# Windowed attention and a gated MLP: two pairs of heads together, scores in three bursts, values in two

## The chip, the cores and the metric

The kernel runs on one core of one Trainium2 chip. The metric is the time on the device in microseconds (us) of one execution. Five engines work beside each other: TensorE (PE in the profile, its weight loads PEld), VectorE (DVE), ScalarE (ACT), GpSimd (POOL) and SyncE (SP, which here issues all loads and stores). Each runs its own instructions in order and waits for the others by semaphores.

## What is computed

Causal attention over a window of 128 keys with a slope per head, then an MLP whose second half is mixed over the sequence. Shapes: 8 batches, 8 heads, 576 positions, 64 dimensions a head; d_model 512, d_ff 1024. All in float32.

```python
scores = q @ k.T / sqrt(64) - slope[h] * |i - j|   # where 0 <= i - j < 128
attn = softmax(scores); x = attn @ v               # heads side by side: (8, 576, 512)
h = gelu_tanh(x @ w_in); u, v = halves of h
v_n = (v - mean) / sqrt(var + 1e-6) * g_ln         # over the 512 features
v_s = w_sg @ v_n + b_sg                            # over the 576 positions
out = x + (u * v_s) @ w_out
```

## The kernel before

*Attention, by pair of heads* (class Pair, 32 pairs, four to a batch). Queries are cut into 18 groups of 32. A group n needs the keys of five groups, n-4 to n, which are 160 columns; groups 0 to 3 need fewer. PE is used in tiles. For the scores, tiles of 64 rows (the 64 dimensions of one head) by 32 columns (the queries of a group): eight at a time, four groups ("quarters" g of the 128 output partitions) of both heads. For the values, tiles of 32 rows (32 keys, one quarter) by 64 columns (the dimensions of one head), eight as well. A pair has nine slots, each holding one group in each quarter: slots 0 to 4 (X) and 5 to 8 (Y); the first slot of each has the early groups 0 to 3 with 128 columns (padded with a bias), the others 160.

The steps of pair n, by the letters of the order below: `q` loads q and k, `L` loads v (five transfers a pair); `*` 36 score products into four banks of PSUM (72 matmuls in the trace, where each fp32 product of these tiles appears twice); `A B C G` on DVE subtract from the bias and take the row minimum (L281); `e E f F` exponentials on ACT with their sums (L286); `R` reciprocals; `s S` scaling on POOL (L297); `t T` transposes by 32 x 32 blocks on DVE (L301); `V` 80 value products, one for each group of 32 keys, quarter and head, with one to five groups of 32 queries as columns (160 matmuls, L331), into four banks; `x` copies the result to xf, `h l k` split it into a high and a low part (xs). The probabilities of a pair stand in one of three buffers e; qk and vt have two buffers each. A pair's score burst (`*`) and value burst (`V`) are each issued without a break.

*The MLP, by batch.* u and v from w_in (`u`, `v`, `tt`), normalisation (`n..`), mixing over the sequence (`y`, L687, L688), gating (`gm gh gl`), w_out (`O`, L540 to L542) and the sum with x (`oa`), store (`D`). Each product is three matmuls (high x high, high x low, low x high) on the whole array, of 288 columns or, for v and tt, of 512. A step of u or O has 12 matmuls, of y 14, of v 12 and of tt 8. The weights are split once at the start (`i d b + H -` and `w..`); `i` loads a quarter of a half of w_in or w_out.

*The order.* A planner collects every step with its engine, its needs and its buffers; the order in which the steps are issued is written out by hand (`ORDER`), and each engine follows it. ON_VECTOR names those copies and subtractions that DVE does instead of ACT or POOL. In the old order PE begins `*0 *1 *2 V0 *3 V1 *4 V2 *5`, then the first `v` of batch 0 between `V3`, `*6` and `V4`; it ends with `V31 V30` and the last MLP.

## Time and profile before

| | |
|---|---|
| median of 3 runs | 643.37 us (637.86 to 644.07) |
| the profiled execution | 642.52 us, its span 640.8 us |
| mean granted TensorE clock | 0.947 of full speed |
| busy: PE, PEld, DVE, ACT, POOL | 587.4, 541.0, 376.6, 355.0, 231.0 us |
| moved by DMA | 59.37 MB, mean 93 GB/s |

The span runs from the first to the last instruction of the profiled execution; its own time is 1.7 us more. Busy times count an engine's instructions, not its waits. Matmuls overlap in the records, so a start-to-start distance tells more than the length of one. "issue" as the reason of a wait means that the engine waited for nothing that the profile shows. [...]

### The profile page before, as it was taken

What the parts mean: (1) busy time and instruction counts of PE and PEld (TensorE: products, weight loads), DVE (VectorE), ACT (ScalarE), POOL (GpSimd) and SP (SyncE); (2) the same over time, 40 slices, a digit from 0 to 9 for tenths busy, and PEclk for the clock granted to TensorE, in tenths of its full rate; (3) what the DMA queues carried; (4) which work ended last, traced back from release to release, by engine and by line L of the source; (5) the groups of instructions that cost most, each with busy time, mean ns of one, the idle gap of its engine ahead of it and who ended that gap; (6) DMA issues with size and microseconds to landing.
All of it is one profiled execution on the core that took longest, in us unless ns stands there. A gap on an engine that the chain in (4) does not pass through costs nothing.

```text
span 640.8 us, 23707 instructions
## 1 busy us (share of the span) xinstructions
PE 587.4 (92%) x10304; PEld 541.0 (84%) x10304; DVE 376.6 (59%) x1211; ACT 355.0 (55%) x951; POOL 231.0 (36%) x197
## 2 busy tenths in 40 slices
PE   4569979999999999899989999999798998989997
PEld 3457867999998899797988999888797997988997
DVE  7668995377566676456736763547273466534422
ACT  6765968676452673558535874387281843512320
POOL 7666484174233212321612532424050542141020
PEclk9669998999999999899989999999697998979999
DMA  9984544501532323222324053432522022300103
GB/s 259 244 240 125 174 115 115 112 2 40 160 114 62 100 84 120 78 62 82 102 49 105 3 179 100 95 68 68 132 86 71 1 59 68 80 3 1 38 1 112
DMA packets 57564, 59.37 MB, mean 93 GB/s; under 512 B 4466, under 2 KB 47474, under 8 KB 57460
## 3 DMA queue, kind: packets, MB, share of 16 engines
q1 hardware_dynamic: 57460, 57.86, 33.0%
q8 instruction: 81, 1.33, 0.9%
q14 instruction: 23, 0.19, 0.1%
HBM read 48.40 MB, written 9.44 MB: 90 GB/s over the span
## 4 chain that ended last, share of the span: by engine, by line
PE 89%; issue 6%; DVE 1%; ACT 1%; POOL 1%; DMA 1%; POOLq 0%; SPq 0%; ACTq 0%
PE bank L540 22%; PE bank L541 21%; PE bank L542 21%; PE bank L331 13%; PE bank L266 8%; PE bank L688 1%; PE bank L687 1%; PE bank L623 1%; PE bank L625 1%; DMA wst<-w_in 1%; POOL g L702 1%; ACT e L286 1%; DVE e L301 0%; DVE e L281 0%; POOLq L870 0%
## 5 line engine op out<-in xcount | busy, mean ns | idle before, releaser
L286 ACT ACTIVATE e<-e,small 128x160 f32<-128x160 f32 (+1 forms) x288 | 118.0, 411 | 16.4 <-DVE small L281 16.0
L297 POOL TENSOR_TENSOR e<-e,small 128x640 f32<-128x640 f32 (+1 forms) x64 | 91.2, 1443 | 97.0 <-DVE small L290 87.7
L331 PEld LDWEIGHTS bank<-e,vt 32*64 32x64 f32 x5120 | 80.4, 143 | 47.7 <-issue 42.4
L331 PE MATMUL bank<-e,vt 32*64 32x32 f32 (+3 forms) x5120 | 86.5, 252 | 37.3 <-issue 30.4
L281 DVE CUSTOM_DVE_ANT_0 e<-bank,bias 128x160 f32<-128x160 f32 (+1 forms) x288 | 74.6, 308 | 23.0 <-PE bank L266 22.6
L564 POOL TENSOR_TENSOR small<-small 128x1 f32<-128x1 f32 (+1 forms) x40 | 30.1, 755 | 150.9 <-DVE small L561 145.8
L540 PE MATMUL bank<-ws,vn 128*128 128x288 f32 x256 | 79.6, 311 | 0.0
L702 POOL TENSOR_TENSOR g<-u,g 128x576 fp32r<-128x576 f32 x32 | 46.8, 1481 | 87.8 <-ACT g L699 87.6
L541 PE MATMUL bank<-ws,vn 128*128 128x288 f32 x256 | 78.0, 305 | 0.0
L542 PE MATMUL bank<-ws,vn 128*128 128x288 f32 x256 | 77.9, 304 | 0.0
L540 PE MATMUL bank<-xs,wi 128*128 128x288 f32 x256 | 77.4, 302 | 0.0
L540 PE MATMUL bank<-g,wo 128*128 128x288 f32 x256 | 76.7, 300 | 0.0
L542 PE MATMUL bank<-xs,wi 128*128 128x288 f32 x256 | 76.4, 298 | 0.0
L541 PE MATMUL bank<-xs,wi 128*128 128x288 f32 x256 | 76.3, 298 | 0.0
L541 PE MATMUL bank<-g,wo 128*128 128x288 f32 x256 | 75.7, 296 | 0.3 <-POOL g L702 0.3
L542 PE MATMUL bank<-g,wo 128*128 128x288 f32 x256 | 75.5, 295 | 0.0
L694 DVE TENSOR_TENSOR u<-bank,u 128x288 f32<-128x288 f32 x64 | 27.8, 448 | 81.1 <-PE bank L688 73.1
L266 PE MATMUL bank<-qk 64*32 64x160 f32 (+1 forms) x2304 | 60.4, 332 | 12.7 <-issue 5.9
L266 PEld LDWEIGHTS bank<-qk 64*32 64x32 f32 x2304 | 46.1, 120 | 21.6 <-issue 10.8
L301 DVE STREAM_TRANSPOSE e<-e 128x608 f32<-128x608 f32 (+1 forms) x64 | 55.7, 879 | 8.7 <-POOL e L297 8.6
L286 ACT ACTIVATION_READ_ACCUMULATOR e<-e,small 128x1 f32 x288 | 54.0, 187 | 0.0
L725 DVE TENSOR_TENSOR xf<-bank,xf 128x288 f32<-128x288 f32 x64 | 27.9, 449 | 41.5 <-PE bank L542 41.3
(97 smaller groups left out, 1312.3 us busy)
## 6 DMA issues: line engine op xcount, KB each, us to landing
qk<-qkT SPq DMA_DIRECT2D x32, 576.0 KB, 5.0
vt<-v_in SPq DMA_DIRECT2D x96, 128.0 KB, 3.4
outT<-xf SPq DMA_DIRECT2D x28, 288.0 KB, 2.3
vt<-v_in SPq DMA_DIRECT2D x32, 176.0 KB, 3.5
wst<-w_in SPq DMA_DIRECT2D x8, 512.0 KB, 6.9
vt<-v_in SPq DMA_DIRECT2D x32, 64.0 KB, 3.9
wst<-w_out SPq DMA_DIRECT2D x4, 512.0 KB, 5.6
wst<-w_sgT SPq DMA_DIRECT2D x4, 288.0 KB, 3.1
```

The lines of the kernel that those rows point to most:

```text
L266: return lambda: nc.tensor.matmul(self.place[s][quarter[g]], qk[heads[j], 0, n * Q:(n + 1) * Q], ks, start=True, stop=True)
L281: nc.vector.tensor_tensor_reduce(out=self.pr[:, s, skip:KW], in0=self.place[s], in1=bs, scale=-1.0 / math.sqrt(D), scalar=3e38, op0=ALU.ad ...
L286: nc.scalar.activation(x, x, AF.Exp, bias=self.nm[:, s:s + 1], scale=-1.0, accum_out=self.sm[:, s:s + 1])
L297: nc.gpsimd.tensor_tensor(x, x, self.rr[:, ss].rearrange("p (m o) -> p m o", o=1).broadcast_to(list(x.shape)), ALU.mult)
L301: nc.vector.transpose(x, x)
L331: insts.append(lambda x=x, at=at, n=len(mine): nc.tensor.matmul(*x, start=(at == 0), stop=(at == n - 1), skip_group_check=True))
L540: nc.tensor.matmul(dst, ah, bh, start=(first and i == 0), stop=False)
L541: nc.tensor.matmul(dst, ah, bl, start=False, stop=False)
L542: nc.tensor.matmul(dst, al, bh, start=False, stop=(last and i == n - 1))
L564: nc.gpsimd.tensor_tensor(x["rs"][0:rows], x["rs"][0:rows], mhalf[0:rows], ALU.pow)
L702: nc.gpsimd.tensor_tensor(st[f"g{f}"][:, 1, :], st["u"][:, f, :], st[f"g{f}"][:, 0, :].bitcast(F32), ALU.subtract)
L725: nc.vector.tensor_tensor(o, st[f"po{c}{i}"][:, 0:S2], o, ALU.add)
```

## The change

Two pairs of heads (a "Two", 16 of them) go through the softmax together. Each quarter g now holds, for one of the two pairs (g // 2), a run of seven groups that follow each other: groups 4 to 10 or 11 to 17. Two sets of slots (base 0 and 1, seven slots each, all of 160 columns) are the two heads. The early groups 0 to 3 of both pairs get four slots of their own (32, 64, 96 and 128 columns) in base 0. That makes 18 slots for two pairs, as before.

- Scores come in three bursts `*a *b *c` (slots 0 to 2, 3 to 5, 6 and the early ones) of 24 products each, 48 matmuls in the trace, two banks each; each burst has its own minima (`Aa Ba` ...), exponentials (`ea Ea` ...), reciprocals, scaling and transposes. The early slots are scaled on DVE (`z`, four operations), no longer on POOL.
- Values come in two bursts: `Va` takes the keys that need only parts a and b (48 products, 96 matmuls), `Vb` the rest (56 products, 112 matmuls). With seven consecutive groups a product has up to five groups of queries for most keys: 104 products for two pairs instead of 160. Both bursts write the same four banks, and the two pairs' `x` copy from them after `Vb`.
- v is loaded in six transfers for two pairs instead of ten. A load of q and k waits for all three bursts of the Two before; only Two 1 gets a buffer of its own, borrowed from vn. There are two buffers e and two vt, each for a Two.
- ON_VECTOR and ORDER are written anew. PE begins `*a0 *c0 *b0 *b1 *a1 *c1 Va0 Vb0 *a2 *b2 *c2`, then a first part of `v`, `Va1 Vb1 *a3 *c3`, the rest of `v` of batch 0, `*b3 tt0 Va2 Vb2 *c4 *b4 *a4`, three `y` and eight `u` steps, `Va3 Vb3`. From Two 4 on, Va and Vb stand next to each other on PE in six of twelve Twos.

The core of the diff; "..." marks what is left out, most of the order among it. Of the functions of Two, which take the place of those of Pair printed above, the new lines alone are shown.

```diff
+    RUN = (S // Q - NG) // 2
+    CUT = (0, 3, 6, RUN)
+    NS = 2 * RUN + NG
+    LATER = 2 * RUN * KW
+    EW = LATER + NG * 3 * Q + Q
...
+    def head_of(base, g):
+        return g // 2 if base == 0 else 1 - g // 2
+    def first_of(g):
+        return NG + g % 2 * RUN
+    def early_pair(g):
+        return (0, 1, 1, 0)[g]
...
+    class Two:
+        def __init__(self, d):
+            self.d, self.b, self.hp = d, 2 * d // NPAIR, 2 * d % NPAIR
+            self.nm, self.sm, self.rr = stats[d % 2]
             self.heads = [slice(j * D, (j + 1) * D) for j in range(2)]
+            self.pr = e_bufs[d % 2]
+            self.bias = biases[self.hp // 2]
+            self.qk, self.to = [None] * 2, {}
+        def load_qk(self, p):
+            if self.d == 1:
+                if p == 0:
+                    self.both = mlp.tile([P, 2, 2, S], F32, name="qk1", tag="vn")
+                x = self.both[:, p]
+            else:
+                x = att.tile([P, 2, S], F32, name="qk", bufs=2)
+            self.qk[p] = x
+            h = 2 * (self.hp + p)
+            nc.sync.dma_start(x, qkT[self.b, h:h + 2].rearrange("h d t s -> (h d) t s"))
         def load_v(self):
+            b, kv = self.b, NG + RUN
+            vt = self.vt = att.tile([P, kv + 2, 2 * D], F32, name="vt", bufs=2)
+            def rows(k, n, c, w):
+                return v[b, k * Q:(k + n) * Q, c:c + w].rearrange("(k p) d -> p k d", p=Q)
             for g in range(NG):
...
+                c0 = (self.hp + g // 2) * 2 * D
+                nc.sync.dma_start(vt[quarter[g], 0:kv], rows(first_of(g) - NG, kv, c0, 2 * D))
+                if g % 2:
+                    c0 = (self.hp + early_pair(g)) * 2 * D + head_of(0, g) * D
+                    nc.sync.dma_start(vt[quarter[g], kv:].rearrange("p i (j d) -> p (i j) d", j=2), rows(0, NG, c0, D))
...
+        def scores(self, k):
+            heads, work = self.heads, range(CUT[k], CUT[k + 1])
             insts = []
+            def score(x, base, g, p, n, keys):
+                j = head_of(base, g)
+                qk = self.qk[p]
+                ks = bass.AP(qk.tensor, qk.offset + S + (n + 1) * Q - keys, [list(qk.ap[0]), [1, keys]])[heads[j]]
+                insts.append(lambda: nc.tensor.matmul(x[quarter[g]], qk[heads[j], 0, n * Q:(n + 1) * Q], ks, start=True, stop=True))
+            at = [bank(), bank()]
+            for base in range(2):
+                for i in work:
+                    self.to[base, i] = at[base][:, (i - CUT[k]) * KW:(i - CUT[k] + 1) * KW]
+            for i in work:
                 for g in range(NG):
+                    for base in range(2):
+                        score(self.to[base, i], base, g, g // 2, first_of(g) + i, KW)
+            if k == 2:
+                c = len(work) * KW
+                for n in reversed(range(NG)):
+                    w = (n + 1) * Q
+                    x = self.to[2, n] = at[0][:, c:c + w]
+                    c += w
+                    for g in range(NG):
+                        score(x, 0, g, early_pair(g), n, w)
             burst(insts)
...
+        def slots(self, base, k):
+            for i in range(CUT[k], CUT[k + 1]):
+                c = (base * RUN + i) * KW
+                s = self.stat(base, i)
+                yield self.to[base, i], self.pr[:, c:c + KW], self.bias[:, base], slice(s, s + 1)
+            if k == 2 and base == 0:
+                for n in reversed(range(NG)):
+                    c, w, s = LATER + n * 3 * Q, (n + 1) * Q, 2 * RUN + n
+                    yield self.to[2, n], self.pr[:, c:c + w], self.bias[:, 2, KW - w:], slice(s, s + 1)
...
         def scale(self, k):
+            n = CUT[k + 1] - CUT[k]
+            x = self.pr[:, 0:LATER].rearrange("p (b i c) -> p b i c", b=2, i=RUN)[:, :, CUT[k]:CUT[k + 1]]
+            r = self.rr[:, 2 * CUT[k]:2 * CUT[k + 1]].rearrange("p (b i o) -> p b i o", b=2, o=1)
+            if n == 1:
+                x, r = x[:, :, 0], r[:, :, 0]
+            nc.gpsimd.tensor_tensor(x, x, r.broadcast_to(list(x.shape)), ALU.mult)
...
+        def early_scale(self):
+            for n in range(NG):
+                c, w, s = LATER + n * 3 * Q, (n + 1) * Q, 2 * RUN + n
+                nc.vector.tensor_scalar(self.pr[:, c:c + w], self.pr[:, c:c + w], self.rr[:, s:s + 1], None, ALU.mult)
...
+            parts = [((b * RUN + CUT[k]) * KW, (b * RUN + CUT[k + 1]) * KW) for b in range(2)]
+            if k == 2:
+                parts[1:] = [(parts[1][0], EW)]
+            for a, z in parts:
+                nc.vector.transpose(self.pr[:, a:z], self.pr[:, a:z])
...
+        def values(self, k):
+            if k == 0:
+                self.x1 = banks(NG)
+            x1, tp, heads = self.x1, self.pr, self.heads
+            cut = CUT[2]
             work = []
...
+            for base in range(2):
                 for g in range(NG):
+                    j = head_of(base, g)
                     mine = []
...
+                    for c in range(NG + RUN):
+                        i0, i1 = max(0, c - NG), min(RUN - 1, c)
+                        if (c >= cut) == k:
+                            mine.append((self.v_of(g, j, c, False), (base * RUN + i0) * KW + (c - i0) * Q, KW - Q, i1 + 1 - i0, i0 * Q))
+                    if k == 1 and base == 0:
+                        for c in range(NG):
+                            mine.append((self.v_of(g, j, c, True), LATER + c * 4 * Q, 3 * Q, NG - c, (RUN + c) * Q))
...
+                x = x1[heads[j], g, o:o + count * Q], vk, along(tp[qs, c:c + Q], step, count)
+                insts.append(lambda x=x, start=(k == 0 and at == 0), stop=(k == 1 and left[i] == 0): nc.tensor.matmul(*x, start=start, stop=stop, skip_group_check=True))
             burst(insts)
...
         def gather(self):
             xf = self.xf = mlp.tile([P, S], F32, name="xf", bufs=2 * NC)
...
+            p = self.n % 2
+            x1, copy = twos[self.n // 2].x1, copier(f"x{self.n}")
+            copy(xf[:, P:S].rearrange("p (i c) -> p i c", i=2), x1[:, 2 * p:2 * p + 2, 0:RUN * Q])
+            for g in range(NG):
+                if early_pair(g) == p:
+                    x = self.heads[head_of(0, g)]
+                    copy(xf[x, 0:P], x1[x, g, RUN * Q:RUN * Q + P])
...
+    def add_two(d):
+        at = pair_at(2 * d)
+        def put(op, engine, length, after, at=at, to=d, **kw):
+            add(f"{op}{to}", where(f"{op}{to}", engine), length, at, lambda: Two.STEPS[op](twos[d]), [x if isinstance(x, str) else name(*x) for x in after], **kw)
+        for p in range(2):
+            n = 2 * d + p
+            take = [("qk", [f"*{c}{d}" for c in "abc"])] if d != 1 else []
+            add(f"q{n}", "SP", 1.75, at - 12.0, lambda p=p: twos[d].load_qk(p), ["q2"] if n == 3 else [], take=take, lag=2.0)
+        put("L", "SP", 3.6, [], at - 2.0, take=[("vt", [f"Vb{d}"])], lag=2.0)
+        free = ("Vb", d - 2)
+        for k, c in enumerate("abc"):
+            put(f"*{c}", "PE", 1.0, [f"q{2 * d}", f"q{2 * d + 1}", free], take=[("ps", [f"{x}{c}{d}"]) for x in "AB"])
+            put(f"A{c}", "DVE", 0.7, [f"*{c}{d}", free])
+            put(f"B{c}", "DVE", 0.7, [f"*{c}{d}", free])
+            put(f"e{c}", "ACT", 1.2, [f"A{c}{d}"], table="e")
+            put(f"E{c}", "ACT", 1.2, [f"B{c}{d}"], table="e")
+            put(f"R{c}", "DVE", 0.34, [f"e{c}{d}", f"E{c}{d}"])
+            put(f"s{c}", "POOL", 1.7, [f"R{c}{d}"])
+            if k == 2:
+                put("z", "DVE", 0.45, [f"R{c}{d}"])
+            put(f"t{c}", "DVE", 1.0, [f"s{c}{d}"] + ([f"z{d}"] if k == 2 else []))
+        put("Va", "PE", 1.45, [f"ta{d}", f"tb{d}", f"L{d}"], take=[("ps4", [f"x{2 * d}", f"x{2 * d + 1}"])])
+        put("Vb", "PE", 1.65, [f"tc{d}", f"Va{d}"])
...
-        put("q", "SP", 1.75, [], -12.0, take=[("qk", [f"*{n}"])], lag=2.0)
-        put("L", "SP", 3.6, [], 3.0 - OPEN / 2, take=[("vt", [f"V{n}"])], lag=2.0)
-        put("*", "PE", 1.6, [f"q{n}", ("V", n - 3)], take=[("ps", [f"{k}{n}"]) for k in "ABCG"])
-        put("A", "DVE", 0.93, [f"*{n}", ("V", n - 3)])
-        put("B", "DVE", 0.93, [f"A{n}"])
-        put("C", "DVE", 0.93, [f"B{n}"])
-        put("G", "DVE", 0.65, [f"C{n}"])
-        put("e", "ACT", 0.8, [f"A{n}"], table="e")
-        put("E", "ACT", 0.83, [f"B{n}"], table="e")
-        put("f", "ACT", 1.22, [f"C{n}"], table="e")
-        put("F", "ACT", 0.83, [f"G{n}"], table="e")
-        put("R", "DVE", 0.34, [f"{k}{n}" for k in "eEfF"])
-        put("s", "POOL", 1.03, [f"R{n}"])
-        put("S", "POOL", 1.28, [f"R{n}", f"s{n}"])
-        put("t", "DVE", 0.75, [f"s{n}"])
-        put("T", "DVE", 0.9, [f"S{n}", f"t{n}"])
-        put("V", "PE", 1.7, [f"T{n}", f"L{n}"], take=[("ps4", [f"x{n}"])])
-        put("x", "ACT", 1.35, [f"V{n}"], take=[("xf", [f"D{b}{c}"] if b < B - 1 else [f"D{b}{c}{i}" for i in range(2)])])
+        put("x", "ACT", 1.0, [f"Vb{n // 2}"], take=[("xf", [f"D{b}{c}"] if b < B - 1 else [f"D{b}{c}{i}" for i in range(2)])])
...
-        tt0 nv20h x6 uc010 vn02 w-0 w-2 h4 V7 tj0 h6 h5 l4 x7 h7 l6 *8 *9 tg0 l5 A8 l7 v11 nt0b A9 wl1 nt0c v10
...
+        *b3 k3 vn00 z2 tl k2 vg03 wl3 wH1 q8 wH0 nv30b H6 nv30p -6 nv30c tt0 tc2 nv30h w-1 wH3 Va2 Vb2 vn03 tj0
...
+        q9 tg0 Ab3 w-0 nt0b tH nt0p t- *c4 x5 nt0c nt0h x4 *b4 *a4 tn0 i7 Bc4 w-3 d7 Bb3 b7 q11 ec3 Ea3 +7 i8
...
+        O120 nv12b D11 x12 oa120 z7 v20 D10 sc7 vg20 nv12c tb7 u221 u201 nv12p x13 ta7 tc7 nv02b q17 Va7 Vb7
...
+        nv02p uc201 nv12h uc210 u211 D13 u220 D12 uc221 uc231 vn21 nv02c x15 x14 *a8 L8 *b8 *c8 h14 nv02h h12
...
```

## Rows read from the trace of the kernel before

**Rows 1.** The page: span, busy time by engine, the instruction queue of part 3.
```profile
span 640.8 us, 23707 instructions
...
PE 587.4 (92%) x10304; PEld 541.0 (84%) x10304; DVE 376.6 (59%) x1211; ACT 355.0 (55%) x951; POOL 231.0 (36%) x197
...
q8 instruction: 81, 1.33, 0.9%
```
**Rows 2.** Windows, two stretches: busy us (and instructions) by engine, clock, DMA share, GB/s.
```profile
0.00:102.84 102.84, 74.85 (x2152) 63.63 (x2152) 79.92 (x263) 72.54 (x226) 64.20 (x64) 0.83 0.65 181
102.84:637.57 534.73, 512.51 (x8156) 477.42 (x8152) 296.18 (x948) 282.45 (x726) 166.76 (x133) 0.97 0.28 75
```
**Rows 3.** Timeline of PE: start us, us, what. An undisturbed score and value burst.
```profile
128.85 0.39 PE L541 MATMUL bank<-wi,xs 128*128 128x512 f32 x1
129.08 0.39 PE L542 MATMUL bank<-wi,xs 128*128 128x512 f32 x1
129.39 1.56 PE L266 MATMUL bank<-qk 64*32 64x128 f32 x72
130.88 0.41 PE L540 MATMUL bank<-xs,wi 128*128 128x288 f32 x1
131.13 0.30 PE L541 MATMUL bank<-xs,wi 128*128 128x288 f32 x1
131.26 0.30 PE L542 MATMUL bank<-xs,wi 128*128 128x288 f32 x1
...
156.34 2.34 PE L331 MATMUL bank<-e,vt 32*64 32x128 f32 x160
158.61 0.40 PE L540 MATMUL bank<-g,wo 128*128 128x288 f32 x1
```
**Rows 4.** Groups by line and form: count | busy us, mean ns of one | idle before.
```profile
L540 PE MATMUL bank<-ws,vn 128*128 128x288 f32 x256 | 79.6, 311 | 0.0
...
L540 PE MATMUL bank<-wi,xs 128*128 128x512 f32 x128 | 51.3, 401 | 0.0
...
L687 PE MATMUL bank<-wsA,vA 128*128 128x288 f32 x64 | 19.4, 304 | 0.0
...
L623 PE MATMUL bank<-wi,xs 128*128 128x512 f32 x32 | 9.0, 403 | 0.0
```
**Rows 5.** Chain of waits from 254.84 us: start us, us, what.
```profile
254.84 1.49 PE bank L266 x72
256.33 0.40 PE bank L331 x11
256.73 0.60 issue
257.33 1.70 PE bank L331 x90
259.03 2.57 issue
```
**Rows 6.** Waits from 102.84 to 577 us: us in total, times, longest us.
```profile
PEld bank L331 <- issue: 24.8, 33, 2.9
```
**Rows 7.** Windows, PE alone: first and last of the six half-clock stretches, and their sum.
```profile
262.50:266.00 3.50, 3.50 (x38) 0.54 0.02 5
...
562.90:569.70 6.80, 6.49 (x128) 0.52 0.01 4
sum 34.10, PE 31.08; mean PE 5.18
```
**Rows 8.** Groups by line and form: exponentials on ACT, scaling on POOL.
```profile
L286 ACT ACTIVATE e<-e,small 128x160 f32<-128x160 f32 x224 | 92.9, 416 | 5.3 <-DVE small L281 5.1
...
L297 POOL TENSOR_TENSOR e<-e,small 128x800 f32<-128x800 f32 x32 | 50.2, 1572 | 0.0
...
L297 POOL TENSOR_TENSOR e<-e,small 128x640 f32<-128x640 f32 x32 | 42.0, 1315 | 97.0 <-DVE small L290 87.7 <-ACT u L669 8.8 <-PE bank L331 0.4
```
**Rows 9.** Tile qk: its loads, from issue to landing.
```profile
DMA to landing us min/median/max: 3.8/5.0/8.9
```

## The prediction

> **What bounds the kernel now.** The page comes first: TensorE (PE) is busy for 587.4 of the span's 640.8 us [rows 1]. Then the windows view: until 102.84 us PE is busy 74.85 us and the DMA engines 65%; from there to its last matmul, 512.51 of 534.73 us, with every other engine below 300 [rows 2]. So PE sets the end, and what counts is its own work plus what holds it up. Its work is added up from undisturbed stretches [rows 3] and counts [rows 4]. A 288-column matmul follows the last after 0.134 us, a 512-column one after 0.23; an undisturbed score burst takes 1.49 us to the next matmul (129.39 to 130.88), a value burst 2.27 (156.34 to 158.61). Nine groups of 256 and two of 64 with 288 columns, three of 128 and two of 32 with 512: 2,432 x 0.134 + 448 x 0.2275 = 427.8 us. 32 score bursts are 47.7, 32 value bursts 72.6. Together 548.1 us; the rest of the span is loss.

> Up to 102.84 us PE has done 10 score and 8 value bursts, 56 wide and 96 narrow matmuls: 14.9 + 18.2 + 12.7 + 12.9 = 58.7 us, so the filling of the pipeline loses 44.1. After it stand 489.4 us of work in 534.7: a loss of 45.3. The chain of waits shows where: inside a run of score and value bursts PE stops twice with nothing released, 0.60 and 2.57 us, 1.70 us of matmuls apart [rows 5]. The page gives the likely reason: queue q8 brought 81 packets and 1.33 MB of instructions, while PE issued 20,608 matmuls and weight loads, that is 254 for each 16 KB packet, or 127 matmuls. A value burst spends 127 matmuls in 127 x 14.2 ns (2.27 us / 160) = 1.8 us; a stall follows where a second packet's end falls into one run of small matmuls. The view of waits after 102.84 us books 24.8 us on this [rows 6]. [...]

> [...]

> **The change, part by part.** *Value bursts.* A pair's 80 products of the program are 160 matmuls in the trace (each appears twice); two pairs now have 104 instead of 160 products, so 208 matmuls instead of 320, with the same 320 blocks of 32 x 32. By the cadence of 14.2 ns, Va (96) costs 1.36 us and Vb (112) 1.59. By columns: the score burst streams 768 columns (128 + 4 x 160) through its fullest tile in 1.49 us, 1.94 ns each; Va's fullest tile has 640, Vb's 800: 1.24 and 1.55, the lower bound, 2.8 together. The upper bound takes the old value burst as going by columns: 768 in its fullest tile in 2.27 us, so 4.26. I take 3.1, a little over the cadence, because Vb is uneven (early groups only in four of eight tiles). Scores with as many columns need only 1.49, so columns are not what makes 2.27. 16 x 3.1 = 49.6 instead of 72.6: -23.0 us (bounds -27.8 and -4.5).

> *Score bursts.* Three of 48 matmuls instead of two of 72. In each the fullest tile streams 480 columns: 0.93 us by the rate above; with some 0.2 us to enter and leave tiles, 1.0. 16 x 3.0 = 48.0 against 47.7: +0.3 (lower bound 0.93, -3; upper bound 1.49 each as if a burst cost the same at any size, +24).

> *Stalls.* I count runs of score and value bursts without MLP matmuls between them, after the stretch compared above. An unbroken run of n holds (n - 127) / 127 second packet ends on average. Old order from *10: 17 of 160, one of 304, three of 392, the rest 72: 12.1. New order from *c5: six of 208 (Va and Vb adjacent), three of 144, the rest 112 or less: 4.2. By this 24.8 becomes 8.7; runs with only 12 to 28 MLP matmuls between them will stall in part, so I take 12 (bounds 0 and 25): -12.8. The clock's loss goes along, 16.4 x 12 / 24.8 = 8: -8.4.

> *Filling.* In the new order the same PE work (58.6 us: 15 score bursts, four Va and Vb, 56 wide, 138 narrow matmuls) is reached at the end of Vb3. Up to there it holds the same kinds of steps on VectorE and ScalarE as the old one up to *9 (softmax of eight pairs and a part of the next ones, the weights of the first layer, the first MLP steps), so I leave their busy time at 79.9 and 72.5 us [rows 2]. What may improve is the idle time beside it: two pairs load V in six transfers instead of ten. VectorE without any idle time, from 6 us on, gives 86, the lower bound; the old idle time, 103, the upper. I take 95: -7.8. One wait is added here: q8 and q9 wait for *b3 in SP's queue, behind them i7, and so the first u matmuls; this is inside the bounds.

> *Waits.* Two pairs now share one chain, and the two e and two vt buffers hold four pairs each (three and two before), but come free by two pairs at a time. Between the last score burst of a Two and its Va stand over 20 us of PE work from Two 4 on, while one part's chain is some 6 us of instructions (three exponentials of 0.42, a scale of 960 columns at 1.57 + 160 x 0.0016 = 1.83 [rows 8], and shorter ones on VectorE); I allow 6 us in all for new waits (0 to 20).

> *At nothing.* GpSimd's scaling falls from 5.8 us for two pairs (twice 1.57 + 1.32) to two of 1.83 and one shorter, the early groups move to VectorE in four short operations; exponentials stay at 18 for two pairs. All lie under PE, which has the longest busy time by 200 us; if PE waited for them instead, see the fourth rival. The loads of q and k: the buffer is now free only when all three bursts of a Two are done, so the next Two's two transfers must land between. The PE work in the order between that release (or the step that holds SP's queue before it) and the first burst that reads is 4.8 us for Two 4, and 10.1 to 40 for the others. One lands in 5.0 us, at most 8.9 [rows 9], so two lie hidden save for up to 4 us at Two 4, in the filling.

> **Sum.** Against the profiled execution's 642.5 us (span 640.8 and 1.7 around it): -23.0 + 0.3 - 12.8 - 8.4 - 7.8 + 6 = -45.7, so 597 us. The median of the runs, 643.4, lies 0.9 above the profiled one, which I leave out.

> **Rivals.** (1) *Value bursts go by columns.* Then two pairs save 0.28 instead of 1.44 us, 18.5 less in all: 616. For it: fewer, wider products with the same columns. Against: the score burst's 1.49 us. 0.12.

> (2) *No stalls are left*, as each burst but the adjacent ones is shorter than a packet: 597 - 12 - 8 = 577. Against: six adjacent pairs of Va and Vb. 0.12.

> (3) *As many stalls as before*: each of the six adjacent pairs and the runs around them catches a packet's end. 12.8 + 8.4 come back: 618. For it: the same rate of small matmuls, just after each other. 0.13.

> (4) *No change*: PE's saved time turns into waits for the coarser chain, as ScalarE and VectorE are busy 282 and 296 us of 535 [rows 2] and each Two brings its work in lumps. All 45 us would have to return, 3.8 a Two over twelve: about 640. Against: the 20 us of lead. 0.05.

> (5) *Slower: q and k come too late.* With no second pair of buffers each Two starts its loads only after the last Two's bursts. The leads from Two 4 on are 4.8, 25, 40, 12, 16, 22, 10, 19, 10, 12, 13 and 12 us. If the second transfer lands after 17 us, the shortfalls add up to 45 us and the gain is gone; at 20 us to 71, so 668. For it: SP's queue is in order, outputs and V loads stand between. Against: the largest landing of 8.9. 0.08.

> **Chances and range.** The forecast has 0.50 (583 to 612 alone, from the bounds on filling and waits). The range reaches to rival 2 below, and past rivals 1 and 3 above: 577 to 626, which leaves out about 2 in 10. One per cent, 6 us, is about what a measurement of this kernel can tell from no change. Faster by more: forecast and rivals 1 to 3, 0.87; within: 0.05; slower: 0.08.

> **What would show it.** Right: an undisturbed Va near 1.4 and Vb near 1.7 us to the next matmul, score bursts near 1.0; the wait "issue" before the value matmuls near 12 us and stretches at half clock near 17 us in all; Vb3 ending near 95 us. Wrong: Va and Vb over 4 us together (1), waits for q and k before score bursts (5), PE waiting for VectorE before Va (4). The prediction fails most easily by the filling and by new waits, both taken from sums and not from a row.

## The result, and the profile after

The changed kernel takes 603.45 us (median of four runs, 600.4 to 606.7) beside 641.64 us for the kernel before on the same chip: a ratio of 0.941, 95% interval 0.934 to 0.948. Six more runs, beside other runs of the kernel before, gave 0.942 (0.938 to 0.946). Ratios and intervals leave out runs more than 1.5% above the fastest of the same kernel (below these are one run of the kernel without early scaling, and five of six of the shifted old kernel, which therefore has no ratio); medians are of all runs. The forecast was 597 us, so 6 us too low. The profiled execution, read below, has a span of 602.0 us; the forecast's own span, less the 1.7 us around it, was 595.3.

The page after, with the lines that answer to [rows 1]:

```profile
span 602.0 us, 20016 instructions
...
PE 552.1 (92%) x8512; PEld 508.1 (84%) x8512; DVE 398.0 (66%) x1309; ACT 342.7 (57%) x940; POOL 207.9 (35%) x174
...
q8 instruction: 66, 1.08, 0.8%
```

PE has 1,792 matmuls and 35 us of busy time less, and 15 of 81 instruction packets are gone. PE still sets the end.

The windows of after, parted at the end of Vb3, where the forecast parted it (columns as in [rows 2]):

```profile
0.00:109.90 109.90, 75.74 (x1746) 63.71 (x1746) 89.02 (x318) 77.13 (x242) 56.86 (x53) 0.84 0.59 169
109.90:598.84 488.94, 476.40 (x6772) 444.39 (x6766) 308.54 (x990) 265.59 (x700) 151.04 (x121) 1.00 0.24 64
```

This is the main reading. Vb3 ends at 109.9 us and not at 95: the filling is 15 us longer than forecast, and 7 longer than the old one for the same PE work [rows 2]. From there to the span's end it is 492.1 us; the forecast left 500. So two errors of opposite sign, +15 and -8, make the 6.7 us by which the span is longer than forecast, and that the total came within 1% is in part luck.

Undisturbed bursts in the timeline of PE (start us, us, what), for [rows 3]:

```profile
188.91 1.05 PE L264 MATMUL bank<-qk 64*32 64x160 f32 x48
189.89 0.40 PE L582 MATMUL bank<-ws,vn 128*128 128x288 f32 x1
...
220.82 1.57 PE L358 MATMUL bank<-e,vt 32*64 32x160 f32 x96
222.32 0.40 PE L582 MATMUL bank<-g,wo 128*128 128x288 f32 x1
...
224.10 1.87 PE L358 MATMUL bank<-e,vt 32*64 32x160 f32 x112
225.90 0.40 PE L582 MATMUL bank<-xs,wi 128*128 128x288 f32 x1
```

From start to the next matmul's start: scores 0.98, Va 1.50, Vb 1.80 us.

What PE waited for from 110 to 600 us (us in total, times, longest):

```profile
PE bank L583 <- issue: 4.0, 4, 1.7
PE bank L584 <- issue: 3.4, 3, 1.5
PE bank L358 <- issue: 1.5, 2, 1.0
PE bank L665 <- DVE xs L395: 1.3, 1, 1.3
```

and the same view of before, from 102.84 to 577 us:

```profile
PE bank L331 <- issue: 18.8, 12, 2.8
PE bank L266 <- issue: 3.0, 3, 2.1
```

The stalls without a releaser fall from 21.8 to 8.9 us, and they have moved: out of the value bursts into the first MLP matmuls behind them (L583, L584). The other waits of this stretch add up to 3.7 us, the longest 1.3 (before, there were none). No wait for q and k is left here.

The one stretch at half clock after 86 us (for the six of [rows 7]):

```profile
321.70:325.10 3.40, 3.40 (x17) 3.40 (x16) 1.61 (x2) 1.39 (x3) 1.42 (x1) 0.53 0.37 86
```

It loses 0.47 x 3.4 = 1.6 us. A second profile of the same kernel has no such stretch there.

In the filling, one of VectorE's groups up to 109.9 us is new:

```profile
L319 DVE TENSOR_SCALAR e<-e,small 128x32 f32<-128x32 f32 (+3 forms) x16 | 8.2, 574 | 0.0
```

L319 is z, the scaling of the early groups that came over from GpSimd: 16 operations, 8.2 us. The chain that ended last, 40 to 51 us, shows a second thing:

```profile
40.22 2.90 PE bank L358 x63
43.12 4.42 issue
47.54 3.22 PE bank L358 x96
50.78 0.62 DVE xf L380
```

Va1 and Vb1 run at half clock with a stop of 4.4 us near the end of Va1, and VectorE and ScalarE wait for both to gather Two 1.

### The profile page after: what moved, and what is told of

Its sections match the earlier page's. It is cut to its first block, busy times and chain, and to the rows that moved or that the text cites. A ratio compares the mean times of both kernels' runs of the same rounds, so it can differ in the third digit from the quotient of the medians.

```text
span 602.0 us, 20016 instructions
## 1 busy us (share of the span) xinstructions
PE 552.1 (92%) x8512; PEld 508.1 (84%) x8512; DVE 398.0 (66%) x1309; ACT 342.7 (57%) x940; POOL 207.9 (35%) x174
## 4 chain that ended last, share of the span: by engine, by line
PE 76%; DVE 13%; ACT 5%; issue 4%; POOL 1%; DMA 1%; SPq 0%; ACTq 0%
PE bank L582 20%; PE bank L584 19%; PE bank L583 19%; PE bank L358 8%; PE bank L264 5%; DVE e L297 2%; ACT e L301 2%; PE bank L730 1%; PE bank L729 1%; DVE vg L609 1%; DMA wst<-w_in 1%; DVE e L326 1%; POOL g L744 1%; PE bank L665 1%; DVE small L601 1%
## 5 line engine op out<-in xcount | busy, mean ns | idle before, releaser
L301 ACT ACTIVATE e<-e,small 128x160 f32<-128x160 f32 (+4 forms) x288 | 115.2, 402 | 13.3 <-DVE small L297 13.0
L314 POOL TENSOR_TENSOR e<-e,small 128x960 f32<-128x960 f32 (+1 forms) x48 | 70.4, 1477 | 61.8 <-DVE small L306 35.5
L582 PE MATMUL bank<-ws,vn 128*128 128x288 f32 x256 | 78.1, 305 | 0.9 <-DVE u L736 0.9
L584 PE MATMUL bank<-ws,vn 128*128 128x288 f32 x256 | 76.2, 298 | 2.0 <-issue 2.0
L583 PE MATMUL bank<-ws,vn 128*128 128x288 f32 x256 | 76.2, 298 | 2.0 <-issue 2.0
L584 PE MATMUL bank<-xs,wi 128*128 128x288 f32 x256 | 75.5, 295 | 1.5 <-issue 1.5
L583 PE MATMUL bank<-g,wo 128*128 128x288 f32 x256 | 75.4, 295 | 1.0 <-issue 1.0
L583 PE MATMUL bank<-xs,wi 128*128 128x288 f32 x256 | 75.4, 295 | 1.0 <-issue 1.0
L582 PE MATMUL bank<-xs,wi 128*128 128x288 f32 x256 | 76.3, 298 | 0.0
L297 DVE CUSTOM_DVE_ANT_0 e<-bank,bias 128x160 f32<-128x160 f32 (+4 forms) x288 | 69.7, 297 | 9.2 <-PE bank L264 9.1
L584 PE MATMUL bank<-g,wo 128*128 128x288 f32 x256 | 75.4, 295 | 0.0
L358 PEld LDWEIGHTS bank<-e,vt 32*64 32x64 f32 x3328 | 55.2, 138 | 18.9 <-issue 14.0
L358 PE MATMUL bank<-e,vt 32*64 32x160 f32 (+4 forms) x3328 | 58.8, 270 | 13.0 <-issue 10.4
L744 POOL TENSOR_TENSOR g<-u,g 128x576 fp32r<-128x576 f32 x32 | 47.7, 1504 | 63.2 <-ACT g L741 36.2
L264 PE MATMUL bank<-qk 64*32 64x160 f32 (+4 forms) x2304 | 55.4, 310 | 13.3 <-DMA qk<-qkT 8.6
L264 PEld LDWEIGHTS bank<-qk 64*32 64x32 f32 x2304 | 44.6, 115 | 22.4 <-DMA qk<-qkT 9.0
L767 DVE TENSOR_TENSOR xf<-bank,xf 128x288 f32<-128x288 f32 x64 | 27.7, 448 | 47.7 <-PE bank L584 47.5
L326 DVE STREAM_TRANSPOSE e<-e 128x480 f32<-128x480 f32 (+1 forms) x96 | 54.4, 609 | 0.2 <-POOL e L314 0.2
```

What stands on the lines that cost most here:

```text
L264: insts.append(lambda: nc.tensor.matmul(x[quarter[g]], qk[heads[j], 0, n * Q:(n + 1) * Q], ks, start=True, stop=True))
L297: nc.vector.tensor_tensor_reduce(out=e, in0=x, in1=bs, scale=-1.0 / math.sqrt(D), scalar=3e38, op0=ALU.add, op1=ALU.min, accum_out=self.nm ...
L301: nc.scalar.activation(e, e, AF.Exp, bias=self.nm[:, s], scale=-1.0, accum_out=self.sm[:, s])
L314: nc.gpsimd.tensor_tensor(x, x, r.broadcast_to(list(x.shape)), ALU.mult)
L326: nc.vector.transpose(self.pr[:, a:z], self.pr[:, a:z])
L358: insts.append(lambda x=x, start=(k == 0 and at == 0), stop=(k == 1 and left[i] == 0): nc.tensor.matmul(*x, start=start, stop=stop, skip_g ...
```

## Experiments: what a value burst costs

**Wide products split.** In `values`, ahead of the sort:

```
mine = [(vk, c + a * step, step, min(3, count - a), o + a * Q)
        for vk, c, step, count, o in mine for a in range(0, count, 3)]
```

> The value products of four and five groups are split into two (3+1, 3+2): 148 products instead of 104 for two pairs, so 296 matmuls instead of 208, over the same columns and with the same output. Theory A (a value burst costs so much per matmul): an undisturbed Va takes 144 x 15.6 ns = 2.25 us instead of 1.50, Vb 152 x 16.1 ns = 2.45 instead of 1.80, 1.4 us more for each of 16, so 22 us more, and some stalls more because 2,816 instructions come on top (11 block ends of 256): about 625 to 640 us. Theory B (a value burst costs by its columns): Va stays near 1.5 and Vb near 1.8 us, the whole within 5 us of 603.

Measured: 657.25 us, ratio 1.021 (1.013 to 1.029). Undisturbed Va and Vb in the timeline of PE:

```profile
235.73 1.87 PE L359 MATMUL bank<-e,vt 32*64 32x96 f32 x144
237.53 0.40 PE L583 MATMUL bank<-g,wo 128*128 128x288 f32 x1
...
419.64 2.17 PE L359 MATMUL bank<-e,vt 32*64 32x96 f32 x152
421.74 0.41 PE L583 MATMUL bank<-ws,vn 128*128 128x288 f32 x1
```

1.80 and 2.10 us to the next matmul: between both theories. The whole is longer than both forecast. 48 matmuls more cost 0.30 us in Va, 40 more 0.30 in Vb, 6 to 7.5 ns each; the rest goes by columns, (1.50 - 96 x 0.00625) / 640 = 1.41 ns for each column of the fullest tile. These two prices, fitted to Va, give 1.83 for Vb (1.80 measured), 0.98 for the score burst (0.98), 1.53 for the old score burst (1.49) and 2.08 for the old value burst (2.27 [rows 3]). So the change's value bursts win mainly by fewer matmuls, but at 6 ns each and not at the 14 of the cadence: 112 fewer make 0.70 us for two pairs and 96 columns fewer 0.14, of 1.24 measured apart (2 x 2.27 less 3.30); the other 0.4 is the misfit of the old burst and stays open.

Yet the bursts explain only 0.6 us x 16, about 10 of the 48 us by which its span (650.3) is longer. Most of the rest is in its waits after 110 us and in what followed them:

```profile
PE bank L359 <- issue: 30.1, 14, 5.3
```

against 8.9 in the kernel after, with stretches at half clock behind the longest (6.8 us each near 392, 412 and 494 us; a mean clock of 0.98 from 120.8 to 640 us, beside 1.00 behind Vb3 in the kernel after), and its Vb3 ends at 121.0 instead of 109.9. Splitting cost far more here in stalls and half clock than in the bursts themselves.

## Experiments: where the stalls come from

Counted in the trace (two instructions for each matmul, and PE's own semaphore instructions), nearly all stalls without a releaser stand where PE has done a multiple of 256 instructions, plus 192 to 194: 21 of 22 in the kernel before, 13 of 15 in the kernel after, and there all nine behind the filling. Such a place is called a block end here. The kernel before has 81 of them and 81 packets of q8, the kernel after 66 and 66. Most of them are passed without a stall; where one stalls, the last block end is mostly near. In the kernel after, behind Va5 and Vb5:

```profile
172.27 2.87 PE L358 MATMUL bank<-e,vt 32*64 32x160 f32 x192
175.07 0.40 PE L582 MATMUL bank<-ws,vn 128*128 128x288 f32 x1
...
175.70 0.29 PE L583 MATMUL bank<-ws,vn 128*128 128x288 f32 x1
177.16 0.30 PE L584 MATMUL bank<-ws,vn 128*128 128x288 f32 x1 [1.16 <-issue]
```

The block ends are at matmuls 2645 (173.18 us, in Va5) and 2773 (177.16, the sixth behind Vb5), counted from 0. The six side-by-side Va Vb all end like this. To tell place from step, the work was moved against the block ends without changing what it computes.

**Shift by 48 matmuls, at *b3.** In `scores`, ahead of `burst(insts)`:

```
if self.d == 3 and k == 1:
    insts += (3 * insts)[:24]
```

> The 24 products of the burst *b3 are issued twice (the same values are written again, while TensorE would wait some 5 us anyhow), so that all later instructions of TensorE sit 96 further on in its stream, and each block end of 256 instructions falls 48 matmuls earlier in the work. Theory A (a stall comes where two block ends fall into less than some 4 us of work): the stalls of the kernel after sit 0 to 8 matmuls behind the six adjacent Va Vb (Two 5, 7, 9, 10, 12, 15; 9.1 us of 11); now the second end falls into the last third of Vb, after 2.0 us of work instead of 2.5, so the stalls move from the MLP matmuls into Vb5, Vb7, Vb9, Vb10, Vb12 and Vb15, 1.9 us each, and those of all Twos from 4 on grow from 11 to 14 to 18 us; the whole 603 to 612. Theory B (a stall belongs to the step behind Vb, its weights or its waits): the stalls stay at the first matmuls behind Vb, with their sizes, and the whole stays within 2 us of 603.

Measured: 609.75 us, 0.948 (0.942 to 0.954). The same stretch of the timeline:

```profile
174.64 2.54 PE L360 MATMUL bank<-e,vt 32*64 32x160 f32 x165
178.68 0.85 PE L360 MATMUL bank<-e,vt 32*64 32x32 f32 x43 [1.50 <-issue]
179.46 0.40 PE L584 MATMUL bank<-ws,vn 128*128 128x288 f32 x1
```

The stall stays at matmul 2773, which is now the 166th of Va5 Vb5. So do those at 3665, 4942 (3.3 us from start to start), 5580, 5963, 6601 and 8005. The view of waits after 110 us:

```profile
PE bank L360 <- issue: 13.8, 10, 3.1
...
PE bank L731 <- issue: 0.5, 1, 0.5
```

That is 14.3 us, forecast 14 to 18. These stalls belong to the place in the stream, not to the step.

**Shift by 112.** The same edit with 56 products instead of 24, and once more with 28 products each at *a2 and *b2:

> 56 products of the burst *b3 are issued once more than needed (the same values again, in a wait of TensorE of 5 us), so that every later block end of 256 instructions falls 112 matmuls earlier in the work, that is 16 later than in the kernel after, counted in blocks of 128. Theory A (two block ends may not come closer than some 3.6 to 4 us): behind the adjacent Va Vb the second end now falls 16 matmuls further into the MLP, some 2 us later, and 1 to 5 us of stalls are left of Twos 4 to 15 instead of 11 (15.4 with a shift of 48). If TensorE's time is what counts there, the whole gains 6 to 9 us, 594 to 598. Theory B (ScalarE and VectorE are so close behind that they take up what TensorE wins, as in the run with Va and Vb taken apart, where 7 us of stalls went and the time did not fall): the stalls fall to 1 to 5 us, new waits for ScalarE's and VectorE's copies appear, and the whole stays above 600.

> The same shift of 112 matmuls, but made at the bursts *a2 and *b2 (28 products more in each), so that it holds in the filling too. There the kernel after stops 4.4 us between Va1 and Vb1, at a block end 89 matmuls into Va1. Theory A: later on as with the shift at *b3. In the filling the end moves to the first matmuls of Vb1; if the stall comes from the 16 KB packet being called for late, while TensorE stood waiting, it stays at some 4 us there, and Vb3 ends where it did, 109 to 112 us; if it comes only from the place, it goes, Vb3 ends 3 to 4 us earlier, and the whole is as much shorter than with the shift at *b3.

Measured: 594.05 us, 0.928 (0.924 to 0.932), and 597.93 us, 0.934 (0.929 to 0.939). PE's waits after 110 us with the shift at *b3:

```profile
PE bank L584 <- DVE u L738: 2.0, 1, 2.0
...
PE bank L360 <- issue: 1.2, 2, 0.8
...
PE bank L584 <- issue: 0.4, 1, 0.4
```

1.6 us of stalls instead of 8.9, and 0.928 instead of 0.941 of the kernel before, some 8 us less, with 112 matmuls of useless work more. In spans: 602.0 less 592.3 is 9.7, of which 7.3 lie behind Vb3 and 2.4 before it. Theory A holds, and TensorE's time counts in full here. With the earlier shift the stop in Va1 and Vb1 stayed, 3.6 instead of 4.7 us from start to start, and stands at the next block end (matmul 860 instead of 732): the place alone does not make it, and its cause stays open.

**Va and Vb taken apart.** In the order, for Two 5, 7, 9, 10, 12 and 15, such as:

```
- u201 ... Va7 Vb7 nv02p uc201 nv12h uc210 u211 D13 u220 D12
+ u201 ... Va7 nv02p uc201 nv12h uc210 u211 D13 u220 Vb7 D12
```

> In the order, 12 to 28 MLP matmuls of the steps next to them are put between Va and Vb of Two 5, 7, 9, 10, 12 and 15, which stood side by side. Nothing else. Theory A (two block ends within some 4 us of work): the second end now comes 1.6 to 3.8 us later, the six stalls behind these Vb (1.45, 1.40, 2.00, 1.75, 1.43, 1.10 us) fall to 0 to 0.5 each, and the whole is 5 to 9 us shorter, 594 to 598. Theory B (TensorE lacks instructions in all, so that what is not lost here is lost at the next dense place): the stalls of Twos 4 to 15 stay near 11 us in all, elsewhere, and the whole within 2 us of 603.

Measured: 608.42 us, 0.947 (0.940 to 0.954): not faster than the kernel after, rather slower. Waits after 110 us:

```profile
PE bank L582 <- ACT u L711: 2.6, 3, 1.6
PE bank L582 <- ACT vg L655: 1.9, 2, 1.7
PE bank L665 <- DVE xs L395: 1.6, 2, 1.3
PE bank L358 <- issue: 1.5, 2, 1.1
PE bank L264 <- DVE u L736: 1.4, 1, 1.4
...
PE bank L583 <- issue: 0.4, 1, 0.4
```

The stalls fell to 1.9 us as theory A had it, but the other waits rose from 3.7 to 11.3: banks that ScalarE and VectorE free too late, probably because everything behind the later Vb comes later. Six bursts no longer side by side cost 6 x 0.18 = 1.1 us more. Neither forecast came true: theory A's stalls went but not its time, and theory B, which had the time at 603 within 2 us, had the stalls stay near 11. The shift takes away as many stalls without the new waits; it leaves the order alone.

**The kernel before, shifted by 80**, with 40 products of pair 9's scores issued twice:

> The kernel before with the same kind of shift: 40 products of the score burst of pair 9 are issued twice (the same values again), so that every later block end of 256 instructions falls 80 matmuls earlier in the work. They cost 0.8 us themselves. The question is whether the gain of the change is the place of the block ends, which the old order could have had too. Theory A (runs of 304 and 392 small matmuls hold two block ends wherever the first one lies): by a cycle of 3.4 to 3.8 us for each block this is the old order's best place but for a few per cent, and stalls of 18 to 21 us are left behind the filling, of 24.8; with the clock that follows them some 5 us are won, a ratio of 0.99 to 0.995. Theory B (the old order sat at a bad place only): stalls below 10 us, a ratio near 0.96.

Its runs lie between 628.4 and 646.9 us (median 639.5, beside 641.6), so the time decides no more than that 0.96 is not reached. Weight-load waits in the value bursts of the profiled run (644.2 us), 102 to 580 us:

```profile
PEld bank L333 <- issue: 21.6, 30, 4.8
```

against 24.8 [rows 6]; by PE's own rows it is 21.9 us beside 21.8 of the kernel before. So in this run the stalls are all still there, though by the estimate above (3.4 to 3.8 us for a block) this was nearly the old order's best place. The run of 628.4 us has no profile, and no other place was tried: that some place would serve the old order much better is not excluded.

## Experiments: the filling

**Four steps to other engines**: h2 and H4 leave the set `ON_VECTOR` for ScalarE, l2 and -5 for GpSimd.

> Four short steps of the filling change engine: the cast h2 and the cast H4 from VectorE to ScalarE, the differences l2 and -5 from VectorE to GpSimd. In the kernel after they take 1.68 + 1.96 + 1.74 + 0.68 = 6.1 us of VectorE between 53 and 61 us. Theory A (VectorE without idle time sets the filling): Vb3 ends 4 to 6 us earlier than 109.9, and the whole is as much shorter, 597 to 600. Theory B (the filling is held by TensorE's own stalls at half clock, 4.4 us between Va1 and Vb1 the largest, or by transfers): Vb3 ends within 1 us of 109.9 and the whole stays near 603. Theory C (ScalarE is as full as VectorE and the exponentials behind the casts come late): Vb3 ends later.

Measured: 601.47 us, 0.936 (0.930 to 0.941), not to be told from the kernel after. Its window up to Vb3:

```profile
0.00:109.40 109.40, 73.84 (x1740) 62.04 (x1742) 82.93 (x314) 77.90 (x243) 59.23 (x55) 0.86 0.62 169
```

6.1 us of VectorE are gone, and Vb3 ends 0.3 us earlier. In this run's chain GpSimd's l3, +4, l2, -5 and sa2 stand between 55 and 62.6 us, where VectorE's steps stood. For these steps theory A does not hold.

**No scaling of the early groups in the first four Twos**: `early_scale` returns at once for `self.d < 4`.

> The scaling of the early groups by VectorE is left out for the first four Twos (their early groups stay without the division by the row's sum); in the kernel after these 16 operations take 8.2 us of VectorE before Vb3's end, 0.57 us each, though one takes 0.12 where GpSimd is idle. Theory A (VectorE's busy time sets the filling, 89 us of it before 109.9 instead of 79.9 before 102.8): Vb3 ends 5 to 8 us earlier, and the whole is 596 to 599. Theory B (the filling is a chain of single steps over VectorE, ScalarE, GpSimd and TensorE's own stalls, in which these operations lie only in part: 2.3 of Two 0 and 0.8 of Two 2 are on the chain that ended last): Vb3 ends 2 to 3.5 us earlier, the whole 600 to 602.

(The 0.12 us in this text is that of a 128x6 operation; the quickest four of L319 take 0.76 us together, 0.19 each.) Measured: 603.23 us, 0.940 (0.932 to 0.949). Up to Vb3:

```profile
0.00:104.90 104.90, 76.08 (x1743) 65.31 (x1744) 82.61 (x302) 75.70 (x241) 56.95 (x53) 0.84 0.64 177
```

In the profiled run Vb3 ends 4.8 us earlier, a little short of theory A (the kernel after itself ends it at 109.9 in one profile and 111.1 in the other); 2.6 of them are given back behind it, where a half-clock stretch near 114 us and a wait of 2.0 us for VectorE's gates are new. The medians show no gain.

**Queue order**: behind Vb1 the exponentials of Two 2 and the weight steps are put ahead of the gathers x3 and x2.

```
- Vb1 *a3 x3 h3 Ec2 x2 sa2 l3 b4 L2 i6 *c3 H5 eb2 w10 +4 w21 h2 l2 L3 -5 w22 ta2 v02 wl1 w11 Eb2 Rb2 sb2 w12 Bc3 ec2 H4
+ Vb1 *a3 Ec2 eb2 Eb2 b4 sa2 H5 Rb2 +4 -5 ec2 ta2 L2 i6 H4 sb2 x3 h3 x2 l3 *c3 w10 w21 h2 l2 L3 w22 v02 wl1 w11 w12 Bc3
```

> The kernel after itself, beside the next two on one chip. Its ratio to the kernel before was 0.941 [0.934, 0.948]; 0.94 again.

> Order only, between Vb1 and w22: in the kernel after, the gathers x3 and x2 of Two 1 stand in the queues of VectorE and ScalarE ahead of eleven exponentials of Two 2 and of the weight steps b4, H5, +4, -5, H4 and the transposition ta2, all of which had their inputs by then; ScalarE idles 8.4 and VectorE 4.3 us until TensorE has done Vb1. Here they stand ahead of x3 and x2. Theory A (queue order: some 3 us of VectorE and 4.5 of ScalarE are done in that idle time instead of behind it): the first Gelu of the MLP, 60.6 us in the kernel after, starts 4 to 6 us earlier, Vb3 ends 3 to 6 us before 109.9, and the whole is as much shorter, a ratio of 0.932 to 0.937. Theory B (that stretch is held by GpSimd, as in the run with four steps on other engines, whose Vb3 ended 0.3 us earlier): Vb3 within 1 us, the ratio 0.94.

Measured: the kernel after 0.942; this order 606.37 us, 0.947 (0.943 to 0.950), slower by 3.6 us in the medians of six runs each on one chip. In its run the stops of PE fell into Vb0 (5.2 us from start to start) and into the burst behind Vb1 (4.1); none stood in Va1 or Vb1, which was done 3 us earlier. Then the gathers, now late in their queues, held PE:

```profile
PE bank L264 <- ACT xf L384: 3.7, 1, 3.7
```

and w10 started 6.1 us later, at 59.5 us. But the second profile of the kernel after itself has its stops in the same two places (6.0 and 5.0 us), and w10 at 58.1. This order, fitted to where one run idled, did not fit the next.

**Together**: this order, tb0 ahead of z0 and the shift of 112; and the last two alone.

> The order of the run before, tb0 ahead of z0 in VectorE's queue (z0 takes 2.3 us there, beside GpSimd, and only Vb0 needs it), and the shift by 112 matmuls at *b3. If the gains add up: 9.7 us of the shift and 3 to 6 of the filling against the kernel after, 588 to 591 us and a ratio of 0.916 to 0.925. If ScalarE and VectorE set the pace behind the filling: no more than the shift alone, 0.928.

> The kernel after with the shift of 112 matmuls at *b3 and with tb0 ahead of z0 in VectorE's queue, without the other edits to the order of the filling. If z0's 2.3 us stood ahead of Va0 alone: Va0 starts 2 us earlier, Vb3 ends 1 to 2 us earlier than with the shift alone (107.3), a ratio of 0.924 to 0.928. If the stop at a block end in Vb0 or Va1 takes it up: 0.928 as with the shift alone.

Measured: 595.03 us, 0.930 (0.926 to 0.933), and 594.17 us, 0.928 (0.923 to 0.933). Nothing that can be told from noise is won beyond the shift. The kernel after with the shift at *b3 is the fastest version here: 0.928 of the kernel before, beside 0.942 of the kernel after.

## Why the prediction was right or wrong

**What bounds the kernel**: right. PE ends the kernel, and its stalls behind the filling count in full (the shift of 112: 7.3 us of stalls less, 7.3 us of span behind Vb3 less).

**Values, -23.0**: right in size, wrong in reason. 3.30 us apart and 3.12 side by side, forecast 3.1: about -21 for 16. The cadence of 14.2 ns is no constant: the split shows a sum of matmuls and columns, the columns being the larger part (0.9 of Va's 1.5 us). That 3.1 came out all the same is in part luck. The reason against rival 1, that scores with as many columns take only 1.49 us, was sound.

**Scores, +0.3**: 0.98 alone and 0.90 in a row of two, forecast 1.0; 2 us better. The 0.2 us to enter and leave tiles can be read in [rows 3]: the burst starts 0.31 us after a 512-column matmul, 0.08 more than 0.23, and the second matmul behind it 0.25 us after the first, 0.12 more than 0.134.

**Stalls, -12.8**: right. 21.8 to 8.9 us by PE's rows is -12.9. The forecast went from 24.8 to 12 by the rows of PE's weight loads in the value bursts, and named that view as its sign; there the kernel after has

```profile
PEld bank L358 <- issue: 4.4, 16, 1.2
```

because most stalls now come behind the value bursts, not in them. The mechanism stands: ends of 256-instruction blocks, in six side-by-side pairs and the work behind them. What a count averaged over all places could not give is that this order's own place mattered: 1.6, 8.9 or 14.3 us by a shift alone. So rivals 2 and 3 point at other places in the same stream more than at other mechanisms, though no place tried brought rival 3's 24.8 us, and the one with almost no stalls took 594 us and not rival 2's 577.

**Clock, -8.4**: too small; 1.6 us are left, -14.8. The 16.4 us it starts from are what the six stretches of [rows 7] lose, 0.48 x 34.1; the loss was taken as proportional to the stalls. But behind the filling the kernel before has seven stalls of 1.7 to 2.8 us (as the view of waits counts them), with the six stretches at half clock at or behind them, and none behind its shorter stalls. The kernel after has a single stall that long, 1.7 us, with a stretch behind it. It is no sharp line: in its second profile a stall of 1.8 us has none, and in the 48 shift one of 3.1 has one and one of 1.9 does not. Fewer and shorter stalls cost more than proportionally less clock here: 1.6 beside 16.4 us, with stalls of 8.9 beside 21.8.

**Filling, -7.8**: wrong in sign, and outside its own bounds of 86 to 103: +7. The step that failed is that VectorE's busy time stays at 79.9 and only its idle time shrinks. It is 89.0, and the idle time is 20.9 beside 22.9. Of the 9.1 us, 8.2 are z (the other groups rise and fall against each other), which the prediction put at nothing as "four short operations" under PE's cover; in the filling PE covers nothing (it is busy for 75.7 of the 109.9 us, VectorE for 89.0). Nor are they short there: at 0.76 us for four the 16 would take 3.0 us, and the other 5 are lost where GpSimd runs beside them (last section). Leaving z out brings 4.8 us of Vb3's end back, in one profile. The rest of the 15 us stays open: VectorE's load alone isn't it (6 us moved to GpSimd and ScalarE won 0.3, as GpSimd became the chain), and the tried queue order won nothing. PE's own stops are not more than before: without a releaser 9.2 us up to Vb3 (12.8 in the second profile) beside 14.5 in the old filling, and 34.1 us at half clock in both. But single stops are longer, up to 4.4 us (5.8 in the second profile) beside 2.9, and four pairs at a time wait for them; how much the coarser steps cost was not isolated.

**New waits, +6**: 3.7 us for other engines are seen behind the filling, and no wait for q and k: rival 5 is out, and 4.

So the sum: 595.3 forecast, +14.9 filling, -6.4 clock, -0.1 stalls, -2.4 scores, -2.3 waits, +2 values, which is 601; 1 us of the 602.0 is put down to nothing.

## What to carry to other kernels

Cost a stage by its own bottleneck: work moved at nothing onto an engine that is idle on average is not free in the stretch where that engine is full (here 8.2 us of z on VectorE in the filling). Where runs of small matmuls draw stalls without a releaser, as here, count instructions in blocks of 256: moving the block ends by 112 useless matmuls in a wait won some 8 us here, moving them by 48 lost some 4, and both left the order untouched, while the reorderings tried won nothing.

## What the hardware showed unexpectedly

**VectorE beside GpSimd.** The same four operations of L319 take 0.76 us at 74 us, 2.33 at 22.3 and 3.73 at 98.6:

```profile
22.34 2.33 DVE L319 TENSOR_SCALAR e<-e,small 128x32 f32<-128x32 f32 x4
...
98.62 3.73 DVE L319 TENSOR_SCALAR e<-e,small 128x32 f32<-128x32 f32 x4
```

while GpSimd runs

```profile
22.45 0.72 POOL L314 TENSOR_TENSOR e<-e,small 128x320 f32<-128x320 f32 x1 [0.40 <-DVE small L306]
23.13 1.28 POOL L195 TENSOR_TENSOR wi<-vg,wi 128x512 fp32r<-128x512 f32 x1
...
98.39 3.54 POOL L314 TENSOR_TENSOR e<-e,small 128x960 f32<-128x960 f32 x2
```

Of all 64 operations of L319 in the kernel after, the 46 beside which GpSimd does nothing take 0.25 us on average, the 14 beside which it works throughout 1.01. The minima of 160 columns, which read a bank, take 0.32 us with and without it. Why L319 is slowed and the minima are not, no run shows; the trace shows the price, up to 3.0 us for four operations in the filling (3.73 less 0.76).
